# Threshold attention with an ELU feed-forward: an earlier reciprocal, other places for the q and k transposes, and weight sums built later

## The chip, the cores and the metric

The kernel runs on one core of one Trainium2 chip. All data are fp32. The metric is the device time of one execution in microseconds (us); the time before is the median of three runs. The profile is of one further execution, whose span on the core is 1440.2 us. Differences inside the profile carry over to the device time; the two are not the same number.

The engines are called by the profile's short names: PE is the matrix engine (TensorE) and PEld its weight loads, DVE is VectorE, ACT is ScalarE, POOL is GpSimd, and SP issues the transfers. Each engine works through its own list of instructions in the order in which the program put them there. An instruction waits on semaphores for what it needs from other engines, and everything behind it on the same engine waits with it.

## The reference

An attention with a threshold is followed by a feed-forward with an ELU between its two products.

```python
def _attn_ref(q, k, v, tau):                      # q, k, v: (8, 8, 576, 64) fp32, tau = 0.02
    scale = 1.0 / np.sqrt(q.shape[-1])
    scores = scale * np.matmul(q, k.transpose(0, 1, 3, 2))
    thresh = np.max(scores, axis=-1, keepdims=True) - tau
    scores = np.where(scores >= thresh, scores, -1000000000.0)
    scores = scores - np.max(scores, axis=-1, keepdims=True)
    attn = np.exp(scores)
    attn = attn / (np.sum(attn, axis=-1, keepdims=True) + 1e-09)
    return np.matmul(attn, v).astype(np.float32)

# bridge: (B, H, S, D) -> x of (4608, 512)
def _moe_ref(x, w_in, w_out):                     # w_in (512, 2048), w_out (2048, 512), fp32
    h = x @ w_in
    g = np.where(h > 0.0, h, 1.0 * (np.exp(np.minimum(h, 0.0)) - 1.0))
    return (g @ w_out).astype(np.float32)
```

For each row of the scores only the entries within tau of the row's maximum are kept. They are exponentiated and divided by their sum plus 1e-9.

## The kernel before

The attention is cut into 32 pairs of heads and each pair into five steps: four of 128 queries for both heads, and a fifth for the last 64 queries of both heads together. That makes 160 steps, numbered from 0. The program has four stages:

- Steps 0 to 34 are attention, with the conversion of the weights and the first feed-forward units between them.
- Steps 35 to 44 (below, the **middle stage**) run plain feed-forward units beside the attention, and prepare sums and differences of weight blocks for what follows.
- Steps 45 to 159 (the **main stage**) run the attention of one batch beside the feed-forward of the batch before. The products of the feed-forward use Strassen's scheme: 7 block products instead of 8, on sums and differences of blocks. A *first product* computes two blocks of hidden units from `w_in`; a *second round* multiplies the hidden units with `w_out`. Four first products fill one pair of heads, and the second round that belongs to them fills the next pair.
- After the last step only feed-forward is left.

In the main stage the program holds an agenda. `at(t, f)` puts an operation at a planned time, `on_pe(cost, f)` lets the planned clock run on with the matrix work, and the order of planned times becomes the order of instructions on each engine. Planned times are in us, and the hardware doesn't see them. This is one attention step of the main stage:

```python
        def exp_of(pr, i, h):
            st = open_steps[pr, i]
            nc.scalar.mul(st["nb"][:, h : h + 1], st["mx"][:, h : h + 1], nkeep)
            e = att.tile([P, 2, HALF], FP32, name="e")
            nc.scalar.activation(e, st[h][:, :, :HALF], AF.Exp, bias=st["nb"][:, h : h + 1], scale=keep)
            st[h] = st[h], e

            sc, e = st.pop(h)
            wv = st["w"][:, h * S : (h + 1) * S].rearrange("p (a n) -> p a n", a=2)
            nc.vector.scalar_tensor_tensor(wv, sc[:, :, :HALF], st["th"][:, h : h + 1], e, ALU.is_ge, ALU.mult,
                                           accum_out=st["sm"][:, h : h + 1])

        def sums_of(pr, i, hs):
            st = open_steps[pr, i]
            cs = slice(hs[0], hs[-1] + 1)
            nc.gpsimd.tensor_scalar(st["sm"][:, cs], st["sm"][:, cs], 1.0, 1e-9, ALU.mult, ALU.add)

        def reciprocal_of(pr, i, hs):
            st = open_steps[pr, i]
            cs = slice(hs[0], hs[-1] + 1)
            nc.vector.reciprocal(st["rs"][:, cs], st["sm"][:, cs])

        begun = [0.0]

        def softmax(pr, i):
            hs = heads_of(i)
            t = begun[0] = clock[0]
            on_pe(1.25, lambda: scores(pr, i, hs))
            turn_at = t + 1.25 + 0.72 * len(hs)
            for h in hs:
                at(t + 1.2 + 0.01 * h, lambda h=h: max_of(pr, i, h))
                at(t + 2.0 + 0.75 * h, lambda h=h: bound_of(pr, i, h))
                at(t + 2.1 + 0.85 * h, lambda h=h: exp_of(pr, i, h))
                at(turn_at + 1.6 + 0.85 * h, lambda h=h: mask_of(pr, i, h))
            if i or pr:
                at(turn_at, lambda: turn_squares(*steps[pr * NB + i - 1]))
            m = turn_at + 1.6 + 0.85 * len(hs)
            at(m, lambda: sums_of(pr, i, hs))
            at(m + 0.1, lambda: run_elus(m))
            at(m + 0.7, lambda: reciprocal_of(pr, i, hs))
            for h in hs:
                at(m + 0.9 + 0.8 * h, lambda h=h: normalize(pr, i, [h]))
            for x in (2.8, 3.8, 5.0):
                at(t + x, lambda: run_extra(0.9))
            if pr + 1 < NP and i in (2, 3):
                at(m + 0.75, lambda: (prep_q if i == 2 else prep_k)(pr + 1))
                at(m + 0.8, lambda: (copy_q if i == 2 else copy_k)(pr + 1))
            if pr + 2 < NP and i in (3, 4):
                at(m + 0.9, lambda: load(pr + 2, ("qm",) if i == 3 else ("km",)))
            if pr + 1 < NP and i == 3:
                at(m + 0.9, lambda: load(pr + 1, ("v",)))
```

`begun` is the planned start of the step, `turn_squares` transposes the weights `w` of the step **before** on DVE and sends them to a scratch buffer in DRAM (`there`), from where `fetch` brings them back two steps later. `normalize` multiplies the masked exponentials with the reciprocal, on POOL, and so has to be over before `turn_squares` of the next step can start:

```python
    def normalize(pr, i, hs):
        st = open_steps[pr, i]
        for h in hs:
            wv = st["w"][:, h * S : (h + 1) * S]
            nc.gpsimd.tensor_scalar(wv, wv, st["rs"][:, h : h + 1], 1.0, ALU.mult, ALU.mult)
...
    def turn_squares(pr, i):
        w = open_steps.pop((pr, i))["w"]
        x = late["x"].tile([P, NT, NCH, T], FP32, name="x", bufs=2)

        def turn_part(c0, src, nc_):
            nc.vector.transpose(x[:, :, c0 : c0 + nc_], src.rearrange("p (c g n) -> p g c n", c=nc_, n=T))

        if i < NC:
            turn_part(0, w[:, :MAIN], NC)
            turn_part(NC, w[:, MAIN : MAIN + P], 1)
            turn_part(NC + 1, w[:, MAIN + P :], NC)
    ...
```

The transposes of q and k for the next pair, and the small copies behind them (`raw` has a single buffer for each of q and k, so the next load has to wait for the transpose):

```python
    def prep_q(pr):
        qT = qkp.tile([P, S], FP32, name="qT")
        nc.vector.transpose(qT, raws[pr]["qm"].rearrange("p j d -> p (j d)"))
        pairs[pr] = [qT, None, qds[pr % NQD]]

    def prep_k(pr):
        kT = pairs[pr][1] = qkp.tile([P, TAIL + S], FP32, name="kT")
        nc.vector.transpose(kT[:, TAIL:], raws[pr]["km"].rearrange("p j d -> p (j d)"))

    def copy_q(pr):
        qT, _, qd = pairs[pr]
        for i in range(2):
            r = slice(i * D, (i + 1) * D)
            nc.gpsimd.tensor_copy(qd[r, i * TAIL : (i + 1) * TAIL], qT[r, MAIN:])


    def copy_k(pr):
        kT = pairs[pr][1]
        nc.gpsimd.tensor_copy(kT[D:, :TAIL], kT[D:, S:])
```

The matrix work between the operations of a step comes in quarters of 0.87 us planned. A pair has 8, 6, 4, 6 and 4 of them in its five steps. What follows a first product (`exp`, `minus`, `elu`) and a second round (`snap`):

```python
            def exp(c):

                if attending[0] and (v < RU - 1 or c) and begun[0] + 0.3 < now[0] < begun[0] + 4.4:
                    at(begun[0] + 4.4, lambda: exp(c))
                    return
                while len(late_elus) > 1:
                    late_elus.pop(0)[1]()
                e = loc["e", c] = late["x"].tile([P, 2 * CT], FP32, name="ge", bufs=2)
                nc.scalar.activation(e, both(c), AF.Exp)
                if c:
                    loc["e1"] = e
                    at(now[0] + 0.75, minus)
                else:
                    nc.scalar.activation(e, e, AF.Copy, bias=-1.0)
                if attending[0] and (v < RU - 1 or c):
                    late_elus.append((now[0] + 0.7 * c, lambda: elu(c)))
                else:
                    at(now[0] + 1.4, lambda: elu(c))

            def minus():
                e = loc.pop("e1", None)
                if e is not None:
                    nc.gpsimd.tensor_scalar(e, e, 1.0, -1.0, ALU.mult, ALU.add)

            def elu(c):
                if c:
                    minus()

                nc.vector.scalar_tensor_tensor(both(c), loc["e", c], 0.0, both(c), ALU.min, ALU.max)
...
                [(0.1, lambda: nc.scalar.copy(h(1, 0), place(1))),
                 (0.55, lambda: pool("t5", lambda: h(1, 0), "u2", ALU.subtract))],
                [(0.85, lambda: add(h(0, 0), 2, "t5")), (1.5, lambda: exp(0))],
                [(0.1, lambda: add(h(1, 1), 0, "s1")), (1.4 if attending[0] else 0.7, lambda: exp(1))],
                [(0.85, lambda: add(h(0, 0), 2, "t5")), (1.5, lambda: exp(0))],
                [(0.1, lambda: add(h(1, 1), 0, "s1")), (1.4 if attending[0] else 0.7, lambda: exp(1))],
...
            while not all((g, r, c, v) in ready for v in range(2 * k + 2)):   # a second round's quarter k
                ...                                                           # puts the missing elus ahead
            if left[0] == "s":
                need_extra(*((g, r, c, x) for x in range(left[1] + 1)))
            if right[0] == "t":
                need_extra("out")
...
                def snap():
                    loc["s1"] = kept("s1")
                    nc.scalar.copy(loc["s1"], place(0))
...
                    [(0.1, snap)],          # behind block product 0 of a second round; product 2 adds into its bank
```

Weight sums and other work of POOL that has no fixed place stands in a queue `extra`. `run_extra(budget)` takes jobs from its head as long as they cost no more than the budget, and `need_extra` takes all jobs of one kind at once:

```python
    def run_extra(budget):
        while extra and extra[0][0] <= budget:
            cost, _, f = extra.popleft()
            budget -= cost
            f()

    def need_extra(*keys):
        mine = [x for x in extra if x[1] in keys]
        for x in mine:
            extra.remove(x)
            x[2]()
...
        for p in (0, 2):
            extra.extend((1.3, "out", lambda k=k, p=p: one(k, p)) for k in range(3))

    def change_out(u):
        b12, b11 = w_out_sb[:, u : u + 2, HM:], w_out_sb[:, u : u + 2, :HM]
        extra.append((1.3, "out", lambda: nc.gpsimd.tensor_tensor(b12, b12, b11, ALU.subtract)))
...
    with tc.manual_schedule():
        after = []
        make_out(1), make_out(0)
        for n in range(SWITCH, MIDDLE):
            ...
            run_extra(2.7)
            ...
        finish_units(after, slice(0, None))
        assert not units and not pending
        for u in range(0, NU, 2):
            change_out(u)
        need_extra("in")
```

`make_out(r)` is six additions or subtractions of 128x512 blocks for one half of `w_out` (their results `t` go to DRAM and, for the half made last, also stay in SBUF). `change_out` then alters four blocks of `w_out` in place. The sums of hidden units (`sums`, cost 0.8) are appended to the same queue.

Of the kernel before, what the change touches and what calls it, by code (L numbers as in the profile page):

```python
# [14 lines left out]
ALU = mybir.AluOpType  # L15
# [4 lines left out]
def kernel(  # L20
# [397 lines left out]
# [5 lines that stand above are left out]
# [323 lines left out]
    with tc.manual_schedule():  # L746
        after = []
        make_out(1), make_out(0)
# [40 lines left out]
        assert not units and not pending  # L789
        for u in range(0, NU, 2):  # L790
            change_out(u)
        need_extra("in")
# [33 lines left out]
        def first_product(g, u):  # L826
# [44 lines left out]
            def exp(c):  # L871
# [8 lines left out]
                if c:  # L880
                    loc["e1"] = e
                    at(now[0] + 0.75, minus)
                else:
                    nc.scalar.activation(e, e, AF.Copy, bias=-1.0)  # L884
                if attending[0] and (v < RU - 1 or c):
                    late_elus.append((now[0] + 0.7 * c, lambda: elu(c)))
                else:
                    at(now[0] + 1.4, lambda: elu(c))
# [207 lines left out]
        def sums_of(pr, i, hs):  # L1096
            st = open_steps[pr, i]
            cs = slice(hs[0], hs[-1] + 1)
            nc.gpsimd.tensor_scalar(st["sm"][:, cs], st["sm"][:, cs], 1.0, 1e-9, ALU.mult, ALU.add)

        def reciprocal_of(pr, i, hs):
            st = open_steps[pr, i]
            cs = slice(hs[0], hs[-1] + 1)
            nc.vector.reciprocal(st["rs"][:, cs], st["sm"][:, cs])  # L1104
# [3 lines left out]
        def softmax(pr, i):  # L1108
# [4 lines left out]
            for h in hs:  # L1113
                at(t + 1.2 + 0.01 * h, lambda h=h: max_of(pr, i, h))
                at(t + 2.0 + 0.75 * h, lambda h=h: bound_of(pr, i, h))
                at(t + 2.1 + 0.85 * h, lambda h=h: exp_of(pr, i, h))
# [4 lines left out]
            at(m, lambda: sums_of(pr, i, hs))  # L1121
            at(m + 0.1, lambda: run_elus(m))
            at(m + 0.7, lambda: reciprocal_of(pr, i, hs))
            for h in hs:
                at(m + 0.9 + 0.8 * h, lambda h=h: normalize(pr, i, [h]))
            for x in (2.8, 3.8, 5.0):
                at(t + x, lambda: run_extra(0.9))
            if pr + 1 < NP and i in (2, 3):
                at(m + 0.75, lambda: (prep_q if i == 2 else prep_k)(pr + 1))
                at(m + 0.8, lambda: (copy_q if i == 2 else copy_k)(pr + 1))  # L1130
            if pr + 2 < NP and i in (3, 4):
                at(m + 0.9, lambda: load(pr + 2, ("qm",) if i == 3 else ("km",)))
# [112 lines left out]
```

## Time and profile before

| | before |
|---|---|
| device time, median of 3 | 1453.27 us (1452.48 to 1454.18) |
| span of the profiled execution | 1440.2 us |
| PE busy | 1354.2 us (94%) |
| DVE busy | 1040.8 us (72%) |
| POOL busy | 853.4 us (59%) |
| ACT busy | 633.4 us (44%) |
| instructions | 21812 |
| first and last row maximum of the main stage | 318.8 and 1195.1 us |
| `w_out` sums on POOL (`make_out`, 12) | 243.0 to 282.6 us, 1.27 us each |
| `change_out` on POOL (4) | 362.0 to 365.7 us, 1.27 us each |

The first part of the profile's page gives busy times of the engines; a second part cuts the span into 40 slices. Busy time of PE is modelled at the end of each matrix product, so a PE that is shown busy may still have a small gap. The view of waits names for each engine what ended its idle time; the timeline lists the instructions of an engine in order of time, with the idle time just before an instruction in square brackets; a view of windows gives busy times and granted PE clock in chosen stretches. "L274" is line 274 of the kernel. The lines of main interest are 274 (`normalize`), 348 (transposes of `w`), 195 and 200 (transposes of q and k), 207 and 212 (the copies behind them), 718 and 728 (`make_out`, `change_out`), 847 (first products), 869 (the additions ahead of `exp`), 879 to 899 (`exp`, `minus`, `elu`), 995 (second rounds), 1000 (`snap`), 1078 to 1104 (thresholds, exponentials, masks, sum and reciprocal of a step).

### The profile page before, as it was taken

How to read it: one execution, taken by the hardware profiler on the slowest of the kernel's cores; microseconds unless marked ns; L12 is line 12 of the kernel's file. 1: busy time of each engine (PE TensorE's matmuls, PEld its weight loads, DVE VectorE, ACT ScalarE, POOL GpSimd, SP SyncE). 2: the span in 40 equal slices, each digit the busy share in tenths (PEclk: the TensorE clock that was granted, in tenths of full speed). 3: DMA queues.
4: the chain of work that ended last, by engine and by line, in shares of the span. 5: the costliest groups of instructions: out<-in, count | busy, mean ns of one | idle time of the engine just before them, and what ended most of it. 6: DMA issues, size and time to landing. Idle time of an engine off the chain costs nothing.

```text
span 1440.2 us, 21812 instructions
## 1 busy us (share of the span) xinstructions
PE 1354.2 (94%) x6566; PEld 985.6 (68%) x6566; DVE 1040.8 (72%) x2247; ACT 633.4 (44%) x1387; POOL 853.4 (59%) x1446
## 2 busy tenths in 40 slices
PE   6897989999899999999999999999999999999997
PEld 4455646646576777676767677777767677887886
DVE  6778885977677877788788777877778774545443
ACT  5576664225353544445353535353534452322311
POOL 5567774865657564766476657665575655424422
PEclk9999999999999999999999999999999999999999
DMA  5254442898588889788888878897988885321311
GB/s 110 56 108 144 126 123 52 231 273 238 159 231 220 244 221 233 216 241 223 231 234 216 233 204 244 227 257 209 243 215 240 217 239 163 117 66 48 103 56 30
DMA packets 316629, 260.60 MB, mean 181 GB/s; under 512 B 208352, under 2 KB 272352, under 8 KB 316512
## 3 DMA queue, kind: packets, MB, share of 16 engines
q1 hardware_dynamic: 316512, 259.21, 66.3%
q8 instruction: 53, 0.87, 0.3%
q14 instruction: 64, 0.52, 0.1%
HBM read 168.62 MB, written 90.51 MB: 180 GB/s over the span
## 4 chain that ended last, share of the span: by engine, by line
PE 50%; DVE 15%; POOL 11%; ACT 8%; issue 7%; DMA 5%; SPq 3%; DVEq 0%; POOLq 0%; ACTq 0%
PE f L995 21%; PE f L847 11%; PE sc L238 7%; PE pv L388 5%; DVE x L348 2%; POOL w L274 2%; ACT ge L879 2%; DVE mx L1074 2%; DMA there<-x 2%; PE f L435 2%; POOL s L936 2%; DVE w L265 2%; PE pv L384 2%; POOL ge L893 1%; ACT e L253 1%
## 5 line engine op out<-in xcount | busy, mean ns | idle before, releaser
L274 POOL TENSOR_SCALAR w<-w,rs 128x576 f32<-128x576 f32 x288 | 229.5, 802 | 85.4 <-DVE rs L1104 46.8
L348 DVE STREAM_TRANSPOSE x<-w 128x512 f32<-128x512 f32 (+1 forms) x350 | 185.1, 571 | 36.3 <-POOL w L274 35.8
L238 PE MATMUL sc<-kT,qT 64*128 64x288 f32 x1024 | 184.5, 441 | 23.4 <-DVE w L265 13.0
L1074 DVE TENSOR_REDUCE mx<-sc 128x1 f32<-128x576 f32 x207 | 146.7, 745 | 65.3 <-PE sc L238 65.3
L1084 ACT ACTIVATE e<-sc,nb,keep 128x576 f32<-128x576 f32 x207 | 172.2, 832 | 6.9
L1082 ACT ACTIVATE nb<-mx,nkeep 128x1 f32<-128x1 f32 x207 | 60.9, 294 | 252.9 <-DVE mx L1074 252.8
L1093 DVE SCALAR_TENSOR_TENSOR w<-sc,th,e 128x576 f32<-128x576 f32 x207 | 163.9, 811 | 8.4 <-DVE t L1004 0.2
L238 PEld LDWEIGHTS sc<-kT,qT 64*128 64x128 f32 x1024 | 102.6, 191 | 88.9 <-issue 52.1
L847 PE MATMUL f<-xt,sw 128*128 128x256 f32 x512 | 129.6, 389 | 5.5 <-DMA sw<-win_sums 2.5
L847 PE MATMUL f<-xt,w_in_sb 128*128 128x256 f32 x512 | 128.3, 386 | 6.4 <-ACT w L861 5.5
L995 PE MATMUL f<-w_out_sb,g 128*128 128x256 f32 x448 | 111.6, 388 | 20.1 <-DVE g L899 11.9
L879 ACT ACTIVATE ge<-g 128x512 f32<-128x512 f32 x112 | 70.7, 631 | 110.8 <-DVE g L869 98.5
L847 PEld LDWEIGHTS f<-xt,sw 128*128 128x128 f32 x512 | 93.0, 189 | 35.5 <-issue 15.0
L847 PEld LDWEIGHTS f<-xt,w_in_sb 128*128 128x128 f32 x512 | 93.7, 190 | 32.2 <-ACT w L861 9.8
L995 PE MATMUL f<-t,s 128*128 128x256 f32 x448 | 108.9, 386 | 4.7 <-POOL s L936 4.7
L995 PEld LDWEIGHTS f<-w_out_sb,g 128*128 128x128 f32 x448 | 82.0, 190 | 44.1 <-DVE g L899 16.9
L847 PE MATMUL f<-x,w_in_sb 128*128 128x256 f32 x448 | 109.9, 384 | 1.7 <-ACT g L910 1.7
L253 ACT ACTIVATE e<-sc,nb,keep 128x576 f32<-128x576 f32 x81 | 65.2, 831 | 105.4 <-POOL nb L249 104.4
L899 DVE SCALAR_TENSOR_TENSOR g<-ge,g 128x512 f32<-128x512 f32 x112 | 93.8, 846 | 24.2 <-ACT ge L884 19.9
L995 PE MATMUL f<-w_out_sb,s 128*128 128x256 f32 x448 | 109.6, 387 | 0.9 <-POOL s L936 0.9
L1078 POOL TENSOR_SCALAR th<-mx,ntau 128x1 f32<-128x1 f32 x207 | 54.6, 265 | 74.9 <-DVE mx L1074 74.5
L995 PEld LDWEIGHTS f<-w_out_sb,s 128*128 128x128 f32 x448 | 82.2, 190 | 24.4 <-issue 13.3
(159 smaller groups left out, 2567.6 us busy)
## 6 DMA issues: line engine op xcount, KB each, us to landing
there<-x SPq DMA_DIRECT2D x500, 144.0 KB, 4.2
wTb<-there SPq DMA_DIRECT2D x75, 576.0 KB, 4.8
wTa<-there SPq DMA_DIRECT2D x50, 576.0 KB, 4.3
sw<-win_sums SPq DMA_DIRECT2D x64, 384.0 KB, 4.6
t<-wout_sums SPq DMA_DIRECT2D x45, 512.0 KB, 4.9
qm<-in_q_dram SPq DMA_DIRECT2D x128, 72.0 KB, 4.3
km<-in_k_dram SPq DMA_DIRECT2D x128, 72.0 KB, 4.3
vm<-in_v_dram SPq DMA_DIRECT2D x64, 128.0 KB, 2.9
```

Source lines behind the costliest of these rows:

```text
L238: nc.tensor.matmul(scs[h][:, a, :HALF], qs[r], kT[r, k0 : k0 + HALF], start=True, stop=True)
L253: nc.scalar.activation(e, st[h][:, :, :HALF], AF.Exp, bias=st["nb"][:, h : h + 1], scale=keep)
L274: nc.gpsimd.tensor_scalar(wv, wv, st["rs"][:, h : h + 1], 1.0, ALU.mult, ALU.mult)
L348: nc.vector.transpose(x[:, :, c0 : c0 + nc_], src.rearrange("p (c g n) -> p g c n", c=nc_, n=T))
L388: nc.tensor.matmul(pv[h * D : (h + 1) * D, g0 * T : g1 * T], vm[:, h, c], wT[:, g0:g1, h * (NC + 1) + c], start=False, stop=(c == NC - 1), ...
L847: nc.tensor.matmul(loc["banks"][place], left[:, j], right[:, j], start=(begins and j == 0), stop=(j == 1), skip_group_check=True)
L879: nc.scalar.activation(e, both(c), AF.Exp)
L899: nc.vector.scalar_tensor_tensor(both(c), loc["e", c], 0.0, both(c), ALU.min, ALU.max)
L995: nc.tensor.matmul(place(m), lhs, rhs, start=(begins and v == 0), stop=(v == RU - 1), skip_group_check=True)
L1074: nc.vector.tensor_reduce(st["mx"][:, h : h + 1], st[h][:, :, :HALF], axis=AX.XY, op=ALU.max)
L1084: nc.scalar.activation(e, st[h][:, :, :HALF], AF.Exp, bias=st["nb"][:, h : h + 1], scale=keep)
L1093: nc.vector.scalar_tensor_tensor(wv, sc[:, :, :HALF], st["th"][:, h : h + 1], e, ALU.is_ge, ALU.mult, accum_out=st["sm"][:, h : h + 1])
```

## The change

The change touches only the order and the engine of small operations; what is computed stays.

- The sum's `+ 1e-9` goes from POOL to DVE and stands with the reciprocal right behind the masks. It used to be DVE (mask), POOL (`+ 1e-9`), DVE (reciprocal), POOL (`normalize`). `normalize` is planned 0.6 us earlier.
- The transposes of q and k for the next pair go from the third and fourth step of a pair to the first and third, ahead of or among the normalizations; the copies behind them go behind the normalizations, and the loads of the pair after that follow the transposes.
- Second heads' exponentials are planned 0.2 us later, `minus` 0.85 us later, and the late `elu` of the second chunk 0.5 us later.
- The six weight sums of the first half (`make_out(0)`) are queued at the end of the middle stage, ahead of `change_out`, instead of at its beginning. `run_extra` in the main stage now takes one job per slot whatever it costs; with its budget of 0.9 it took none that costs 1.3.

```diff
--- before.py
+++ after.py
@@ -745,7 +745,7 @@
     MIDDLE = SWITCH + 2 * NB
     with tc.manual_schedule():
         after = []
-        make_out(1), make_out(0)
+        make_out(1)
         for n in range(SWITCH, MIDDLE):
             pr, i = steps[n]
             hs = heads_of(i)
@@ -787,9 +787,10 @@
                     change_in(u)
         finish_units(after, slice(0, None))
         assert not units and not pending
+        need_extra("in")
+        make_out(0)
         for u in range(0, NU, 2):
             change_out(u)
-        need_extra("in")
 
 
 
@@ -879,11 +880,11 @@
                 nc.scalar.activation(e, both(c), AF.Exp)
                 if c:
                     loc["e1"] = e
-                    at(now[0] + 0.75, minus)
+                    at(now[0] + 1.6, minus)
                 else:
                     nc.scalar.activation(e, e, AF.Copy, bias=-1.0)
                 if attending[0] and (v < RU - 1 or c):
-                    late_elus.append((now[0] + 0.7 * c, lambda: elu(c)))
+                    late_elus.append((now[0] + 1.2 * c, lambda: elu(c)))
                 else:
                     at(now[0] + 1.4, lambda: elu(c))
 
@@ -1093,14 +1094,10 @@
             nc.vector.scalar_tensor_tensor(wv, sc[:, :, :HALF], st["th"][:, h : h + 1], e, ALU.is_ge, ALU.mult,
                                            accum_out=st["sm"][:, h : h + 1])
 
-        def sums_of(pr, i, hs):
-            st = open_steps[pr, i]
-            cs = slice(hs[0], hs[-1] + 1)
-            nc.gpsimd.tensor_scalar(st["sm"][:, cs], st["sm"][:, cs], 1.0, 1e-9, ALU.mult, ALU.add)
-
         def reciprocal_of(pr, i, hs):
             st = open_steps[pr, i]
             cs = slice(hs[0], hs[-1] + 1)
+            nc.vector.tensor_scalar(st["sm"][:, cs], st["sm"][:, cs], 1e-9, None, ALU.add)
             nc.vector.reciprocal(st["rs"][:, cs], st["sm"][:, cs])
 
         begun = [0.0]
@@ -1113,23 +1110,22 @@
             for h in hs:
                 at(t + 1.2 + 0.01 * h, lambda h=h: max_of(pr, i, h))
                 at(t + 2.0 + 0.75 * h, lambda h=h: bound_of(pr, i, h))
-                at(t + 2.1 + 0.85 * h, lambda h=h: exp_of(pr, i, h))
+                at(t + 2.1 + 1.05 * h, lambda h=h: exp_of(pr, i, h))
                 at(turn_at + 1.6 + 0.85 * h, lambda h=h: mask_of(pr, i, h))
             if i or pr:
                 at(turn_at, lambda: turn_squares(*steps[pr * NB + i - 1]))
             m = turn_at + 1.6 + 0.85 * len(hs)
-            at(m, lambda: sums_of(pr, i, hs))
+            at(m, lambda: reciprocal_of(pr, i, hs))
             at(m + 0.1, lambda: run_elus(m))
-            at(m + 0.7, lambda: reciprocal_of(pr, i, hs))
             for h in hs:
-                at(m + 0.9 + 0.8 * h, lambda h=h: normalize(pr, i, [h]))
+                at(m + 0.3 + 0.8 * h, lambda h=h: normalize(pr, i, [h]))
             for x in (2.8, 3.8, 5.0):
-                at(t + x, lambda: run_extra(0.9))
-            if pr + 1 < NP and i in (2, 3):
-                at(m + 0.75, lambda: (prep_q if i == 2 else prep_k)(pr + 1))
-                at(m + 0.8, lambda: (copy_q if i == 2 else copy_k)(pr + 1))
-            if pr + 2 < NP and i in (3, 4):
-                at(m + 0.9, lambda: load(pr + 2, ("qm",) if i == 3 else ("km",)))
+                at(t + x, lambda: run_extra(max(0.9, extra[0][0])) if extra else None)
+            if pr + 1 < NP and i in (0, 2):
+                at(m + 0.2, lambda: (prep_k if i else prep_q)(pr + 1))
+                at(m + 1.3, lambda: (copy_k if i else copy_q)(pr + 1))
+            if pr + 2 < NP and i in (0, 2):
+                at(m + 0.9, lambda: load(pr + 2, ("km",) if i else ("qm",)))
             if pr + 1 < NP and i == 3:
                 at(m + 0.9, lambda: load(pr + 1, ("v",)))
```

## The prediction

> **What bounds the kernel now.** I read the page first (busy times and slices), then the windows by stage, the waits of PE in the long stage, and last the timelines around the few places where PE waits. The page:
>
> ```profile
> PE 1354.2 (94%) x6566; PEld 985.6 (68%) x6566; DVE 1040.8 (72%) x2247; ACT 633.4 (44%) x1387; POOL 853.4 (59%) x1446
> ...
> PE   6897989999899999999999999999999999999997
> ```
>
> PE is the bound, and from the twelfth slice on it is close to full. So nothing is won by making POOL or DVE idle more; a gain can only come out of PE's idle time. The windows (PE, PEld, DVE, ACT, POOL busy, then granted clock and DMA share) say how much of it there is:
>
> ```profile
> 400.00:1200.00 800.00, 776.43 (x3884) 569.80 (x3884) 626.80 (x1380) 371.78 (x841) 505.41 (x913) 1.00 0.85 229
> ...
> 361.90:376.50 14.60, 10.49 (x37) 6.97 (x36) 6.42 (x15) 2.73 (x7) 10.33 (x14) 0.77 0.50 136
> ```
>
> 800 - 776.4 = 23.6 us in the bulk of the main stage, and one bad stretch at 362 with 4.1 us of idle PE and a granted clock of 0.77. The waits of PE from 376 to 1200 (total us, times, longest) name the causes:
>
> ```profile
> PE f L995 <- DVE g L899: 9.2, 10, 1.2
> PE f L995 <- ACT s L1000: 7.4, 10, 0.7
> PE f L847 <- DVE g L869: 2.0, 6, 0.4
> PE f L847 <- ACT g L910: 1.7, 4, 0.4
> ```
>
> Two waits, each once per second round, are most of it. Line 899 is the last `elu` before the second half of the first block product, line 1000 the `snap` that has to save a bank before the third product adds into it. The distances between the starts of the matmuls show some 0.16 us more for each than these rows (1.39 for 1.23, 0.91 for 0.74), since ends are modelled; a normal handover is 0.1. How the two arise is seen in one such place (start, duration, engine, line; idle time before in brackets):
>
> ```profile
> 1122.14 0.74 POOL L274 TENSOR_SCALAR w<-w,rs 128x576 f32<-128x576 f32 x1
> ...
> 1122.91 0.71 DVE L348 STREAM_TRANSPOSE x<-w 128x512 f32<-128x512 f32 x1 [1.32 <-POOL w L274]
> ...
> 1127.59 0.63 ACT L879 ACTIVATE ge<-g 128x512 f32<-128x512 f32 x1 [4.26 <-DVE g L869]
> ...
> 1128.92 0.69 DVE L899 SCALAR_TENSOR_TENSOR g<-ge,g 128x512 f32<-128x512 f32 x1 [1.02 <-ACT ge L884]
> ...
> 1129.67 0.70 PE L995 MATMUL f<-w_out_sb,g 128*128 128x256 f32 x2 [0.46 <-DVE g L899]
> ...
> 1132.42 0.36 ACT L1000 COPY s<-f 128x256 f32<-128x256 f32 x1
> ...
> 1132.83 1.35 PE L995 MATMUL f<-w_out_sb,g 128*128 128x256 f32 x5 [0.74 <-ACT s L1000]
> ```
>
> The same timeline shows what stands ahead of the first row: the sum on POOL (line 1099) from 1119.15 to 1119.66, the reciprocal only at 1120.13, as it stands behind two elus on DVE, then on POOL the copy of k at 1121.79, which waited for the transpose of k. So `normalize` starts at 1122.14, 3 us after the sums were there. DVE sits waiting for it in line 348 (1.32 us, and 0.7 once more for the second head), and everything behind on DVE, down to the additions, is late; ACT waits 4.26 us for these, and the elu comes after PE wants it. The snap (1132.42) stands behind the second head's exponential, although its product was over at 1130.4.
>
> **What the Trainium skill says.** "TensorE: Matmul & The Clock Gate", Part 1, says that PE falls to half its clock after an idle window of about 3.4 us. This trace agrees: after the single wait of 3.37 us the clock is 0.77 of full over 14.6 us, which is 0.23 x 14.6 x 2 = 6.7 us at half speed. The same page (Architectural detail) says that ACT, DVE and POOL are strictly first in, first out, and that PE only pulls weight loads ahead; line 348 above, which holds back ready work for 1.32 us, agrees. "VectorE: DVE Perf Modes" (the TRN2 errata) gives about 150 cycles fixed for a DVE instruction; the two-column add and reciprocal of the stages before take a mean of 165 and 160 ns here, so the added add is about 0.16 us.
>
> **The change part by part.**
>
> *A. The snap.* Planned at +3.09 of a second round's step; the second exponential was planned at 2.1 + 0.85 = 2.95, now at 2.1 + 1.05 = 3.15. The order on ACT turns: the snap no longer stands behind a scale and an exponential, 0.29 + 0.83 = 1.1 us. It was 0.7 us late, so the wait should go. Worth 0.91 - 0.1 = 0.8 us each, 12 second rounds start beside attention: 9.6 us. I take 85%, as the snap can slip behind other ACT work: **8.2 us**.
>
> *B. The elu.* Removed from the chain are the hop through POOL (115 times; the op itself 0.32 us mean), the elus ahead of the reciprocal and the copies ahead of `normalize` (on POOL the copies cost 25.3 + 24.9 us of idle time over the run, waiting for the transposes of q and k). `normalize` should start near 1119.5 where it was 1122.14, so DVE's 2 us of waiting in line 348 go, and the transposes of k no longer stand in that step. The elu was at most 1.4 us late. In the timelines its gaps are six of 1.38, four of 0.62, two of 1.05 (the first two) and one of 2.0 at the end of the stage; less 0.1 each: 7.7 + 2.1 + 1.9 + 1.9 = 13.6 us. At 80%: **10.9 us**.
>
> *C. The first second round.* `change_out` is not taken by any slot and is forced in one block just where PE needs sums:
>
> ```profile
> 361.97 5.39 POOL L728 TENSOR_TENSOR w_out_sb<-w_out_sb 128x512 f32<-128x512 f32 x4
> ...
> 368.89 3.96 PE L995 MATMUL f<-t,s 128*128 128x256 f32 x8 [3.37 <-POOL s L936]
> ```
>
> The 3.37 us of waiting go if the ten jobs are done by then. Three slots in each of five steps are 15, ten are needed. With the wait goes the half clock: 6.7 x 0.5 = 3.4 us (eight matmuls took 3.96 us instead of 1.89). 6.8 us at 95%: **6.4 us**.
>
> *D. The small waits of first products* (lines 869, 910 above, and two smaller rows: 2.0 + 1.7 + 0.9 + 1.7 = 6.3 us). Part of them is the same lateness of DVE. At 40%: **2.5 us**.
>
> *E. What is added.* On DVE 115 adds of 0.16 us, 18 us over 880, beside PE: DVE goes from 78% to about 81%, no bound. On POOL, 115 x 0.32 = 37 us less. But in steps 45 to 49 POOL gets 10 x 1.27 = 12.7 us of jobs more (before, they stood at 243 to 283 and at 362). From 318.7 to 361.9 it was busy 26.1 of 43.2 us; now 26.1 + 12.7 - 2 = 36.8, 85%, and over the first 25 us, where three jobs fall in each step, nearly all of it. Thresholds and block sums then queue behind jobs of 1.27 us. Cost on PE: an estimate of **-2 us** from one delay of that size in most of three steps, partly absorbed. One more us for new collisions: **-1**. In the middle stage POOL is relieved of 7.6 us, but PE is full there up to the one wait for a transfer at 298; nothing counted.
>
> Sum: 8.2 + 10.9 + 6.4 + 2.5 - 3 = 25.0 us, 1453.3 - 25 = **1428 us**.
>
> **The rivals.**
>
> *The waits come back in another form.* PE gains some 2% of speed and everything else must follow. DMA is 85% busy in the main stage, and q and k loads now stand earlier among the `there` transfers; if the fetched weights come late, PE waits in line 384. For it: the share of 0.90 in the window from 316 to 360. Against it: all PE waits on DMA from 376 to 1200 are under 2 us. Then 1440 or so.
>
> *POOL becomes the bound in steps 45 to 49.* For it: the 85% above, and FIFO order. If the lag grows to several us, masks come late, scores wait, and the clock may fall once more: +5 to +8 us, 1434 to 1436.
>
> *Everything is only moved.* The elu is early but PE then meets the next late thing, as the margin of the second round is set by ACT (exponentials of attention and of the ELU on one engine). Half of A and B: 1438.
>
> *All of it is had*, and D entirely, with no new costs: 9.6 + 13.6 + 6.8 + 6.3 = 36 us, 1417.
>
> **Range and chances.** 1414 to 1445 us: the low end is the last rival with a little of the handovers, the high end is C and some of A. 2% is 29.1 us, that is 1424.2: four us under my number, a capture of 90% instead of 77% with half of the costs. I give it 0.38. Slower by 2% would need a new wait in every pair of about 1.3 us beyond all gains, which nothing in the profile points to: 0.05. Between: 0.57.
>
> **What would show it.** A: no row of PE waiting for line 1000, and the snap ahead of the second exponential. B: DVE's wait for line 274 (35.8 us) nearly gone, and POOL's waits for the transposes of q and k; the row of line 899 under 3 us. C: line 728 spread over 340 to 362, no wait of 3 us, the clock at 1.00 throughout the main stage. E: POOL over 80% from 318 to 360, with PE idle no more than 4 us there. The prediction is wrong if PE's idle time from 400 to 1200 stays above 12 us, if a DMA or POOL row takes the place of the two, or if the span shrinks by much more than PE's idle time shown, which would mean that handovers counted as busy were waits too.

## The result and the profile after

The change takes the kernel from 1452.88 to 1414.52 us (medians of 4 executions each; one of the kernel before has been added to the three of the table above). The ratio is 0.9735, with a 95% interval of 0.9712 to 0.9758: faster, by 38 us. 1428 was predicted, with a range of 1414 to 1445. The number falls at the lower edge of the range, and the way there differs from the prediction in four of its five terms.

The page after: busy times of the engines, and the slices of PE. (Lines from 789 of the kernel on have moved by one to three: 995 is now 996, 899 is 900, 1000 is 1001, 847 is 848, 1104 is 1101.)

```profile
PE 1342.7 (95%) x6566; PEld 991.3 (70%) x6566; DVE 1059.5 (75%) x2362; ACT 633.4 (45%) x1387; POOL 828.2 (59%) x1331
...
PE   6897989998999999999999999999999999999997
```

PE is still the bound. It has 11.5 us less of busy time for the same 6566 matmuls. As ends are modelled, part of each small wait had been counted as busy. DVE has 115 instructions more and POOL 115 less, as the edit says.

The windows: the bulk of the main stage, steps 45 to 49, and steps 50 to 54 (same columns as in the prediction).

```profile
400.00:1160.00 760.00, 749.95 (x3800) 563.23 (x3799) 629.18 (x1459) 365.17 (x829) 472.13 (x793) 1.00 0.86 235
313.80:359.40 45.60, 40.28 (x186) 28.81 (x184) 34.29 (x63) 21.89 (x51) 38.48 (x54) 0.93 0.91 262
359.40:397.10 37.70, 36.47 (x188) 27.41 (x186) 30.89 (x77) 13.80 (x29) 21.08 (x36) 1.00 0.76 203
```

In the bulk PE is idle for 10.1 of 760 us, where it was 23.6 of 800 (idle time is the stretch less its busy time). Steps 50 to 54, once the bad stretch, now run at full clock. The stretch before them has turned bad: 5.3 us of idle PE, a clock of 0.93, and POOL busy for 38.5 of 45.6 us. The waits of PE from 400 to 1160, all of 0.2 us and more:

```profile
PE f L996 <- DVE g L900: 9.9, 10, 1.2
PE pv L384 <- DMA wTb<-there: 0.2, 1, 0.2
```

The wait for the snap (7.4 us before) is gone, and so are the small waits of the first products. The wait for the elu, 9.2 us before, has stayed whole. That is the plain miss of the prediction.

The best ledger is the starts of the score matmuls (line 238) in PE's timeline, one group per step. Where no wait disturbs it, a step takes the same time from pair to pair to some hundredths of a us, so a part of the change can be seen where it acts. A first-product pair and a second-round pair alternate from step 55 on.

| us in the profile | steps 35-44 | 45-49 | 50-54 | first-product pair, mean | second-round pair, mean | 55-154 |
|---|---|---|---|---|---|---|
| before | 77.8 | 39.0 | 46.9 | 37.81 | 38.27 | 760.7 |
| changed | 74.3 | 45.7 | 37.6 | 36.20 | 37.46 | 736.6 |
| reciprocal alone | 78.8 | 38.9 | 46.8 | 37.21 | 38.17 | 753.8 |
| exponential alone | 81.0 | 37.4 | 46.6 | 37.80 | 37.31 | 751.1 |
| transposes alone | 78.9 | 39.2 | 46.7 | 36.53 | 38.27 | 748.0 |
| weight sums alone | 74.3 | 48.0 | 38.0 | 37.69 | 38.26 | 759.6 |
| changed, transposes back | 74.3 | 47.4 | 37.7 | 38.02 | 37.43 | 754.5 |
| changed, normalizations at once | 74.3 | 44.7 | 37.3 | 36.17 | 36.51 | 726.9 |

The gain in the profiles is 3.6 - 6.7 + 9.3 + 24.2 us in these columns, and 30.7 us in all. The medians differ by 38.4: the profiled execution of the kernel before took 1441.97 us, 11 below its median, that of the changed kernel 1411.32, 3 below its own. So differences inside the profile did not carry over whole to the device time. Of the 8 us between the two, 3 to 5 lie in the set of executions that is compared with: in the three later sets of executions of the kernel before (29, 23 and 7) its median is 1448.2, 1449.5 and 1449.7 us, which makes the gain 34 to 35. What else the other executions of the kernel before had more is in no trace, and stays open; one candidate shows below, in the middle stage.

### The profile page after: what moved, and what is told of

Read it like the earlier page. It is cut to its first block, busy times and chain, and to the rows that moved or that the text cites. A ratio compares the mean times of both kernels' runs of the same rounds, so it can differ in the third digit from the quotient of the medians.

```text
span 1409.5 us, 21936 instructions
## 1 busy us (share of the span) xinstructions
PE 1342.7 (95%) x6566; PEld 991.3 (70%) x6566; DVE 1059.5 (75%) x2362; ACT 633.4 (45%) x1387; POOL 828.2 (59%) x1331
## 4 chain that ended last, share of the span: by engine, by line
PE 67%; DVE 14%; ACT 6%; POOL 6%; issue 4%; DMA 2%; SPq 1%; DVEq 0%; ACTq 0%; POOLq 0%
PE f L996 27%; PE f L848 16%; PE sc L238 10%; PE pv L388 7%; PE f L475 2%; DVE g L900 2%; DVE w L1094 2%; PE f L435 2%; PE pv L384 2%; POOL w L274 2%; DVE w L265 2%; ACT e L1085 1%; ACT ge L880 1%; ACT e L253 1%; PE rt L277 1%
## 5 line engine op out<-in xcount | busy, mean ns | idle before, releaser
L274 POOL TENSOR_SCALAR w<-w,rs 128x576 f32<-128x576 f32 x288 | 243.8, 852 | 114.5 <-DVE rs L1101 75.2
L848 PE MATMUL f<-xt,w_in_sb 128*128 128x256 f32 x512 | 124.7, 382 | 6.0 <-ACT w L862 6.0
L848 PE MATMUL f<-x,w_in_sb 128*128 128x256 f32 x448 | 107.0, 380 | 0.0
L900 DVE SCALAR_TENSOR_TENSOR g<-ge,g 128x512 f32<-128x512 f32 x112 | 88.0, 791 | 25.1 <-ACT ge L885 20.8
```

The costliest lines, as they stand in the source:

```text
L848: nc.tensor.matmul(loc["banks"][place], left[:, j], right[:, j], start=(begins and j == 0), stop=(j == 1), skip_group_check=True)
```

## The experiments

Four kernels have one part of the change each, on top of the kernel before.

**The reciprocal alone.**

```diff
+            nc.vector.tensor_scalar(st["sm"][:, cs], st["sm"][:, cs], 1e-9, None, ALU.add)   # in reciprocal_of
-            at(m, lambda: sums_of(pr, i, hs))
+            at(m, lambda: reciprocal_of(pr, i, hs))
-            at(m + 0.7, lambda: reciprocal_of(pr, i, hs))
-                at(m + 0.9 + 0.8 * h, lambda h=h: normalize(pr, i, [h]))
+                at(m + 0.3 + 0.8 * h, lambda h=h: normalize(pr, i, [h]))
```

> The kernel before with the sum's addition moved to DVE, sum and reciprocal right behind the masks, and the normalizations planned 0.6 us earlier; nothing else. Theory 1 (the hop through POOL is what made DVE and with it the small bank waits of the first products late): the pairs with first products, 37.5 us on the average before, become about 1 us shorter, 11 of them, so -8 to -14 us in all; the 0.91 us wait for the snap and the 1.4 us wait for the last elu in each second round stay. Theory 2 (the place of the q and k transposes did that): at most -4 us here. My prediction on record had the elu wait shrink through this part: -11 us with the row of the elu under 3 us.

Measured: 1442.32 us, ratio 0.9962 (0.9949 to 0.9975). From 55 to 154 it is 6.9 us shorter, 0.6 us in each first-product pair. Of its waits of PE from 400 to 1160 the longest two:

```profile
PE f L995 <- DVE g L899: 8.4, 10, 1.2
PE f L995 <- ACT s L1000: 7.4, 10, 0.7
```

Both waits of the second round stay. POOL's wait for the transposes of k fell from 21.2 to 6.2 us, and DVE's for the normalizations from 30.2 to 21.7, and the elu has next to none of it (8.4 us where it was 9.2). With 5.9 us between the medians and 6.9 in the profile the result lies between the two theories' numbers; the small waits behind line 869 (2.0 us before) are gone, as theory 1 says. It speaks against the prediction, which had put the end of the elu's wait down to the reciprocal.

**The exponential alone.**

```diff
-                at(t + 2.1 + 0.85 * h, lambda h=h: exp_of(pr, i, h))
+                at(t + 2.1 + 1.05 * h, lambda h=h: exp_of(pr, i, h))
```

> The kernel before with the second head's exponential planned 0.2 us later (2.1 + 1.05 h); nothing else. Theory 1: the snap goes ahead of the second exponential, its wait of 0.91 us in 12 second rounds goes, -9 to -10 us, plus up to 2.5 us in the first steps of first-product pairs, where ACT's copies also go ahead of that exponential. Theory 2 (the snap is late because the whole of ACT is late, and the order doesn't matter): under -3 us.

Measured: 1437.39 us, ratio 0.9935 (0.9906 to 0.9964). The second-round pairs are 0.96 us shorter, all of it in their first step (10.62 to 9.60), and no wait for the snap is left. Theory 1. In the first-product pairs the first two steps gain 0.6 us on the mean and the fourth 0.3, but the third loses 0.9: it took 12.72, 11.81 and 9.55 us in three pairs, where 7.77 is normal. The waits of PE from 400 to 1160 name the reason, and the timeline shows what stood ahead in SP's queue in the first of the three:

```profile
PE f L847 <- DMA sw<-win_sums: 7.5, 4, 3.2
...
637.05 2.53 SPq L179 DMA_DIRECT2D km<-in_k_dram  x4
639.68 3.33 SPq L464 DMA_DIRECT2D out_dram<-ot  x2
...
645.82 0.90 SPq L701 DMA_DIRECT2D sw<-win_sums  x1
...
650.65 1.66 PE L847 MATMUL f<-xt,sw 128*128 128x256 f32 x6 [3.22 <-DMA sw<-win_sums]
```

The sums of `w_in` landed late: they were issued 6.2 us after the start of the second step, behind four loads of k and two stores of results. In the changed kernel the transfer of the same pair is issued 0.7 us after that start (627.59), and the four loads, of q there, come behind it (628.91).

**The transposes alone.** The edit is the part of the diff above for prep, copy and load of q and k.

> The kernel before with the transposes, copies and loads of q and k in the first and third step of a pair; nothing else. Theory 1: the copies no longer stand ahead of the normalizations and DVE is freer in the fourth step, which had a wait of 0.4 us in every first-product pair: -2 to -6 us. Theory 2: this carries the shorter first-product pairs: -10 to -14 us.

Measured: 1435.72 us, ratio 0.9919 (0.9898 to 0.994). The first-product pairs are 1.28 us shorter and all ten of their third steps take 7.77 us. Theory 2's number, and twice theory 1's. Of the waits of PE from 400 to 1160, only the two of the second round are left:

```profile
PE f L995 <- DVE g L899: 9.7, 10, 1.2
PE f L995 <- ACT s L1000: 7.4, 10, 0.7
```

**The weight sums alone.** The edit is the part of the diff for `make_out(0)`, `need_extra("in")` and `run_extra`.

> The kernel before with the first half's weight sums queued from step 45 on and one job of any cost taken in each slot; nothing else. Theory 1, from the step times of the changed kernel: steps 35 to 44 get 3.6 us shorter (the store of the sums no longer stands in the queue of SP ahead of the weights' transfers), steps 45 to 49 get 6 to 7 us longer (POOL full, half clock once), step 50 gets 6 us shorter: -2 to -5 us. Theory 2 (POOL bears ten more jobs there at no loss to PE, and the loss in steps 45 to 49 comes from the earlier load of q): -8 to -11 us.

Measured: 1440.5 us, ratio 0.9947 (0.9929 to 0.9965). Steps 35 to 44 gain 3.6 us, steps 45 to 49 lose 9.0, steps 50 to 54 gain 8.9. So moving the jobs away from step 50 costs as much in the pair before, and what is left is the gain in the middle stage: theory 1, by the ledger, whose gains sum to 4.6 us. (The medians lie 7.7 us apart, again more than the profiles show, and close to theory 2's number; but theory 2 had no loss in steps 45 to 49.) How the gain in the middle stage comes about, the timeline of SP's queue shows. The kernel before (first two rows), then PE's row there:

```profile
286.32 2.46 SPq L721 DMA_DIRECT2D wout_sums<-t  x3
288.88 4.13 SPq L361 DMA_DIRECT2D there<-x  x4
...
301.18 0.88 PE L384 MATMUL pv<-wTb,vd 128*128 128x384 f32 x2 [3.16 <-DMA wTb<-there]
```

The changed kernel, which has the same move:

```profile
285.55 2.77 SPq L361 DMA_DIRECT2D there<-x  x4
...
297.49 0.81 PE L384 MATMUL pv<-wTb,vd 128*128 128x384 f32 x2
```

The store of the six sums stood ahead of the transfer of the turned weights. It held it up by some 3 us at its start (288.88 against 285.55, with the two traces 0.37 us apart there), and it took 4.13 us to issue instead of 2.77. PE waited 3.16 us for what came of it. All nine kernels without the store there take 74.3 to 74.5 us for the middle stage, the five with it 77.8 to 81.0. In four of these five the clock also falls to half there, for 3.4 to 6.8 us; in the profiled execution of the kernel before it happens not to. So the move may be worth more in other executions than the 3.6 us of the ledger.

**The late minus and elu alone.**

```diff
-                    at(now[0] + 0.75, minus)
+                    at(now[0] + 1.6, minus)
-                    late_elus.append((now[0] + 0.7 * c, lambda: elu(c)))
+                    late_elus.append((now[0] + 1.2 * c, lambda: elu(c)))
```

> The kernel before with the -1 of the second chunk planned 0.85 us later and its late elu 0.5 us later; nothing else. Theory 1 (these only reorder work with slack): within 2 us of before, -1 to +1. Theory 2 (POOL stands idle for the exponential, 17.7 us in the main stage, with the -1 at its head, and that delays the block sums): -3 to -6 us.

Measured: 1446.77 us, ratio 0.9981 (0.9969 to 0.9993); 761.2 us from 55 to 154, 0.5 more than before. The medians lie 2.7 us apart, between the two theories; by the ledger it is theory 1, and alone this part is worth nothing there. What it is worth inside the change wasn't measured.

Next, the changed kernel with one part back, to see whether the parts add.

**The transposes back.** Everything of the change but the place of the q and k transposes, copies and loads.

> The changed kernel with the transposes, copies and loads of q and k back in the third and fourth step. Theory 1 (each part takes its own waits away, with some overlap of the reciprocal's and the transposes' in first-product pairs): first-product pairs go from 36.2 to 37.0 to 37.3, second-round pairs stay at 37.5, +4 to +6 us from 55 to 155. Theory 2 (with the reciprocal early the copies no longer hold the normalizations, and the transposes' place is worth nothing more): under +1.5 us.

Measured: 1432.2 us, ratio 0.9879 (0.9854 to 0.9905), where the changed kernel has 0.9735; in the profile 17.9 us more than the changed kernel from 55 to 154. First-product pairs take 38.02 us, more than before the change. Both theories are far off (4 to 6, and under 1.5). The first three waits of PE from 400 to 1160:

```profile
PE f L848 <- DMA sw<-win_sums: 9.6, 7, 3.9
PE f L996 <- DVE g L900: 9.5, 10, 1.2
PE f L848 <- ACT g L911: 2.5, 4, 0.6
```

So the transposes' move is worth more inside the change than alone (17.9 against 12.7 us), most likely because the loads of q and k move with them. With the other parts PE arrives earlier at the third step, and in the old place of the loads it meets the `w_in` sums late, as in the run with the exponential alone. This wait for `w_in` sums stands in all six kernels that have the transposes and loads in the old place (one to seven times from 400 to 1160), and in none of the eight that have them in the new one. That it is the order of the loads in SP's queue, and not the load on the DMA engines, is argued from these rows and those of the exponential alone; the loads weren't moved without the transposes.

Then, the elu's wait. In the changed kernel, the timeline ahead of one second round shows why it has stayed:

```profile
574.77 0.17 DVE L1101 RECIPROCAL rs<-sm 128x2 f32<-128x2 f32 x1
...
575.72 0.72 POOL L867 TENSOR_TENSOR u<-u,w 128x256 f32<-128x256 f32 x1 [1.61 <-ACT u L862]
...
576.43 0.74 POOL L274 TENSOR_SCALAR w<-w,rs 128x576 f32<-128x576 f32 x1
577.21 0.71 DVE L348 STREAM_TRANSPOSE x<-w 128x512 f32<-128x512 f32 x1 [1.26 <-POOL w L274]
...
578.44 0.75 POOL L274 TENSOR_SCALAR w<-w,rs 128x576 f32<-128x576 f32 x1
579.22 0.90 DVE L348 STREAM_TRANSPOSE x<-w 128x128 f32<-128x128 f32 x2 [1.30 <-POOL w L274]
```

The reciprocal was over at 574.94, early as planned. But a block sum stands ahead of the first normalization on POOL and waits 1.61 us for ACT, and two more operations stand between the first normalization and the second. DVE waits 1.26 and 1.30 us at line 348, together as long as before the change at the same step:

```profile
589.73 0.71 DVE L348 STREAM_TRANSPOSE x<-w 128x512 f32<-128x512 f32 x1 [1.72 <-POOL w L274]
591.16 0.90 DVE L348 STREAM_TRANSPOSE x<-w 128x128 f32<-128x128 f32 x2 [0.72 <-POOL w L274]
```

**The normalizations at once.**

```diff
-                at(m + 0.3 + 0.8 * h, lambda h=h: normalize(pr, i, [h]))
+                at(m + 0.02 + 0.01 * h, lambda h=h: normalize(pr, i, [h]))
```

> The changed kernel with both normalizations planned directly behind the reciprocal (m + 0.02 and m + 0.03 instead of m + 0.3 and m + 1.1), so that no other work of POOL stands between. Theory 1 (the elu is late because DVE stands 1.3 us twice before the transposes of the step before, waiting for normalizations that queue behind block sums on POOL): the waits of 1.39 and 0.79 us in each second round shrink below 0.3, the first steps of second-round pairs fall from 9.8 to about 8.7, -10 to -13 us from 55 to 155. Theory 2 (the elu is late because of its own chain of additions, two exponentials and the planned lags): within 2 us of the changed kernel. A cost is possible in first-product pairs, whose block sums then stand behind 1.5 us of normalizations: up to +5.

Measured: 1403.03 us, ratio to the kernel before 0.9674 (0.965 to 0.9697). From 55 to 154 it is 9.7 us shorter than the changed kernel, all in the first step of second-round pairs (9.80 to 8.87); first-product pairs lose nothing. The waits from 400 to 1160, of DVE and of PE:

```profile
DVE g L870 <- POOL t L867: 21.0, 22, 2.3
DVE w L1094 <- POOL th L1079: 13.3, 10, 1.3
...
PE f L996 <- DVE g L900: 4.3, 6, 0.7
```

DVE's row for the normalizations (22.1 us in the changed kernel) is gone. Its row for block sums has grown from 3.1 to 21.0 us; these waits lie in first-product pairs, where PE has no wait from them. The elu's wait is gone in four second rounds and 0.7 us in six. That is theory 1, a little under its 10 to 13 us, and it shows that the chain of the prediction was the right one, with the wrong link held to be its bottleneck.

**The threshold earlier as well.** On top of that, in a pair's last step:

```diff
-                at(t + 2.0 + 0.75 * h, lambda h=h: bound_of(pr, i, h))
+                at(t + (1.25 if i == NB - 1 else 2.0 + 0.75 * h), lambda h=h: bound_of(pr, i, h))
```

> The changed kernel with both normalizations directly behind the reciprocal, and in the last step of a pair the threshold on POOL planned 0.75 us earlier. Theory 1 (what is left of the elu's wait, 0.88 us in six second rounds, is DVE standing 1.33 us for a threshold that queues behind three block operations on POOL): the 0.88 us go, the first step of a second-round pair falls from 8.87 to about 8.4 us on the mean, -4 to -6 us from 55 to 155 against the run with the normalizations alone, and the share of the four second rounds that had none stays. Theory 2 (the chain of additions and exponentials itself takes that long): no change from it, within 1.5 us.

Measured: 1401.7 us, ratio 0.9675 (0.9657 to 0.9692), 727.0 us from 55 to 154. Nothing moved, but this doesn't decide: POOL's instructions stand in the same order as without the edit, because no other operation of POOL was planned between the two times. Nor does the row of 13.3 us above say that the threshold is the next link: DVE has this wait of 1.3 us ahead of all ten second rounds, also of the four whose elu is on time. What holds the elu in the other six stays open.

Last, the weight sums.

**The sums early, their store in step 47.** The edit, shortened:

```diff
+        make_out(1), make_out(0)                        # in the middle stage again
-            if (k, p) == (2, 2):                        # store of the sums
+            if (k, p) == (2, 2) and r:                  # that of the first half only in step 47
```

> The changed kernel with the six sums of the first half computed on POOL in the middle stage again, as before the change, but their store to DRAM issued only in step 47; the four in-place changes stay in the slots of steps 45 and 46. Theory 1 (the middle stage lost 3.6 us to the store's place in the queue of SP, not to POOL's work): the middle stage stays at 74.3 us, steps 45 to 49 fall from 45.7 to 37 to 40, steps 50 to 54 stay at 37.6, so -5 to -9 us. Theory 2 (it was POOL's work): the middle stage is back at 77.8 us, -2 to -5 us in all.

Measured: 1413.06 us, ratio 0.9747 (0.9722 to 0.9771): the same as the changed kernel. The middle stage stays at 74.4 us with POOL's work back in it, which settles that the store had cost the 3.6 us, and POOL's work nothing. Steps 45 to 49 take 43.5 us, where theory 1 had 37 to 40: steps 45 to 48 take 30.6 us instead of 38.8. But step 49 takes 12.9 instead of 6.9:

```profile
336.88 2.16 SPq L711 DMA_DIRECT2D wout_sums<-t  x3
...
339.08 5.37 SPq L361 DMA_DIRECT2D there<-x  x4
...
353.45 0.76 PE L384 MATMUL pv<-wTa,vd 128*128 128x256 f32 x1 [3.62 <-issue]
```

The store does the same again, in another place: the transfer behind it takes 5.37 us to issue, PE waits 3.62 us for turned weights (the fetch that depends on that transfer is issued at 348.97 and lands at 353.36), and the clock falls for 6.8 us.

**Both: the normalizations at once and that store.**

> Both of the two edits before in one kernel. Theory 1: their gains add, -15 to -22 us against the changed kernel. If only one of them holds, the gain of that one alone.

Measured: 1402.34 us, ratio 0.9672 (0.9653 to 0.9691). Not above the gain of the normalizations alone.

**The sums early, one store in each of steps 50 to 52, one in-place change in each of steps 45 to 48.** The edit, shortened:

```diff
+            if MIDDLE + NB <= n < MIDDLE + NB + 3:
+                at(clock[0] + 4.5, lambda x=n - MIDDLE - NB: late_store(x))
-                at(t + x, lambda: run_extra(max(0.9, extra[0][0])) if extra else None)
+                at(t + x, lambda x=x: run_extra(1.3 if x == 5.0 and extra and extra[0][1] == "out" else 0.9))
```

> The changed kernel with the first half's sums computed in the middle stage, their three stores issued one in each of steps 50, 51 and 52, and the in-place changes one in each of steps 45 to 48. Theory 1 (steps 45 to 49 lose to POOL's ten jobs, and in the run with the store in step 47 to three stores at once in front of the weights' transfers): the middle stage 74.4 us, steps 45 to 49 fall to 37 to 39, steps 50 to 54 stay under 38.5, -6 to -9 us against the changed kernel. Theory 2 (the loss belongs to the start of the stage itself, as in the kernel before with its 39.0): steps 45 to 49 stay above 41.

Measured: 1414.65 us, ratio 0.9757 (0.9736 to 0.9778). Steps 45 to 49 take 41.1 us, by a hair theory 2's number, and steps 50 to 54 take 40.9, 3 us more than in the changed kernel: PE waited 2.11 us for a block sum in step 50, which stood on POOL behind a normalization that itself waited 1.66 us for DVE. (That the sum came so late because two of three slots had been shut to the larger jobs is argued only.) So 4.6 us won and 3.3 lost. In steps 47 and 48 the five kernels with the six sums in this pair take 9.7 to 11.9 and 8.2 to 10.1 us, the nine without 7.8 to 8.0 and 6.6 to 7.1: that goes with POOL's work there. In step 45 another wait comes first, that for a transfer of `w_in` sums. In the changed kernel:

```profile
318.88 0.45 SPq L701 DMA_DIRECT2D sw<-win_sums  x1
...
324.02 1.19 PE L848 MATMUL f<-xt,sw 128*128 128x256 f32 x2 [2.78 <-DMA sw<-win_sums]
```

This wait is 1.55 us before the change, 2.78 after it, and 0.89, 2.99, 2.54 and 2.36 in the four kernels that have the sums early. Those four have the same order on SP up to there, so this is scatter of the transfers at the beginning of the stage, and a single profile can't tell such a part from a cost of the edit.

**All of it.** The edits of the last kernel, of the normalizations and of the threshold.

> All edits of the two runs before in one kernel. Theory 1: the gains add, -20 to -25 us against the changed kernel, a ratio to the kernel before of 0.957 to 0.962. If the small waits only move, 0.965 or more.

Measured: 1402.95 us, ratio 0.9678 (0.9652 to 0.9704). The sums' new order gives nothing on top, as it gave nothing alone. The version to keep is the changed kernel with the normalizations at once: one line changed, 0.9674 against 0.9735.

## Why the prediction was right, and where it was not

*The bound and where the gain can come from*: right. All of it came out of PE's idle time, and waits of PE told which.

*A, the snap* (8.2 us): right. The exponential alone takes 0.96 us from each of ten second-round pairs, the changed kernel 0.81, that is 8.1 us, and the row of the snap is gone.

*B, the elu* (10.9 us): failed. The row went from 9.2 to 9.9 us. The failed step is "`normalize` should start near 1119.5": it took for granted that POOL would be free as soon as the reciprocal is there. The reciprocal came early, but POOL's queue had other work ahead, which waited itself: the first normalization of the row above starts at 576.43, 1.5 us after the reciprocal's end at 574.94. DVE's waits for line 274, which were to be nearly gone, were 22.1 us from 400 to 1160 (30.2 before). With the normalizations planned at once, 9.7 us came (55 to 154).

*C, the first second round* (6.4 us): right in mechanism, and in size where it was meant, in step 50 (16.27 to 9.97, 6.3 us). The pair gained 9.3 us in all, with 0.8 in step 51 and 2.2 in step 52 (9.99 to 7.82), where two waits went (0.91 and 1.11 us) that the prediction had counted under A and B. The weight sums alone give 8.9 us in this pair, so these too went with them. But "the clock at 1.00 throughout the main stage" was wrong: the fall moved to 323.6.

*D, the small waits of first products* (2.5 us): the right term, sized too low by far. First-product pairs gave 16.1 us in the profile. The step that failed is "at 40%", and, before it, 6.3 us as all there is. The sum of idle rows missed what modelled ends hide (of the 30.7 us by which the span shrank, PE's shown idle time gave 19.2 and its busy time 11.5, which the prediction had named as a sign of being wrong), and nothing in it said that these waits would grow once A was gone: 7.5 us of waits for the `w_in` sums with A alone, 9.6 with all but the transposes. The transposes and their loads took them away.

*E, POOL in steps 45 to 49* (-2 us): the mechanism was foreseen, its size was -6.7 us in the profile. The step "one delay of that size in most of three steps" failed: in steps 47 and 48 alone some 3 us were lost (9.78 for 7.81 and 8.17 for 7.11), and in steps 45 and 46 the late transfer and the half clock came on top. PE was idle for 5.3 us from 318 to 360, where no more than 4 were expected.

*The middle stage* (nothing counted): it gave 3.6 us. The 3.16 us wait for a transfer at 298 was seen and set aside. The prediction hadn't asked what stood ahead of that transfer in SP's queue, and it was a store that the change moves.

In sum: -10.9 for B, -4.7 for E, against +13.6 for D, +2.9 for C, +3.6 for the middle stage and +1 for the collisions that had been set aside. That the number stayed in its range, by half a us, was luck: the misses of B and E cancel those of D, C and the middle stage for the most part, and another 7.7 us lie between the medians and the profiles. Of the ranking of the parts only A and C can be trusted. The rival that DMA would come in the way had the sign of the loads' move wrong: it feared their earlier place, with waits for fetched weights in line 384, but the waits came for `w_in` sums, and only in kernels with the old place. Two smaller slips: 2% would have needed 84% of the gains with half of the costs, (29.1 + 1.5) of 36.3 us, not 90%; and the mean of 165 ns mixes one- and two-column additions, of which the two-column ones took 209.

## What to carry to other kernels

An operation that is made ready earlier gains little while its engine has other work queued ahead: ask of each moved result not when it is there, but what stands before its consumer. Queues of transfers are read in the same way: a store that nobody waits for cost 3 us here because it stood ahead of a load that somebody waits for. And when several waits hide each other, take parts out of the whole change as well as adding them to the old kernel: here one part was worth 12.7 us alone and 17.9 us in company.

## What the runs showed that was not expected

A small addition on DVE can last as long as an addition on POOL beside it. Of the 115 new ones the median is 0.17 us, the longest 1.32. Nine took over 0.3 us, and eight of these ended 0.02 to 0.03 us after an operation of POOL that had begun before them. The longest of the eight:

```profile
344.25 1.27 POOL L728 TENSOR_TENSOR w_out_sb<-w_out_sb 128x512 f32<-128x512 f32 x1
344.47 1.08 DVE L1100 TENSOR_SCALAR sm<-sm 128x2 f32<-128x2 f32 x1
```

The two end at 345.52 and 345.55. The Trainium skill, "GPSIMD Engine Reference", Key points, has GpSimd share its SBUF interfaces with VectorE and names contention with DVE instructions in a 2-port perf mode or with two SBUF inputs. These rows fit such contention, and an addition of two columns isn't always spared; whether it is one of the instructions named isn't shown.

How long a single wait of PE is doesn't settle whether the clock falls. It fell for 6.8 us with the wait of 2.78 us in the changed kernel, and for 3.4 us after one of 2.00 us in the kernel with the normalizations at once. It stayed at 1.00 after one of 3.16 us in the kernel before (at 298) and one of 2.89 us in the kernel with the transposes back (at 943). The windows of 20 us from the start of these four waits, in this order (the clock is the third number from the end):

```profile
321.20:341.20 20.00, 15.74 (x61) 11.14 (x61) 12.44 (x23) 7.78 (x18) 14.46 (x22) 0.83 0.99 286
324.90:344.90 20.00, 16.24 (x71) 11.17 (x72) 13.42 (x25) 9.45 (x21) 16.26 (x24) 0.91 1.01 294
298.00:318.00 20.00, 16.84 (x73) 8.38 (x74) 15.69 (x35) 4.59 (x9) 13.19 (x22) 1.00 0.95 256
943.00:963.00 20.00, 16.70 (x82) 12.16 (x81) 15.08 (x32) 11.07 (x26) 10.72 (x20) 1.00 0.83 266
```

What decides is open.
